# A round trip through DRAM in larger pieces, and a projection one step later, in a fused attention and gMLP kernel

## The chip, the cores and the metric

The kernel runs on one core of one Trainium2 chip. Its engines run side by side and are ordered by semaphores: TensorE (PE in the profile; PEld is its weight load), VectorE (DVE), ScalarE (ACT), GpSimd (POOL) and SyncE (SP), which here only issues DMAs. Every transfer between DRAM and the on-chip memory SBUF goes over the core's 16 DMA engines. TensorE writes to PSUM, which has eight banks. The metric is the device time in microseconds, as the median of several runs.

## The reference

Two branches work on the same layer-normalised input of 2048 rows and 512 columns, and the result is `x + s * silu(B)`. Everything is float32.

```
xn = layernorm(x)
q  = xn @ wq                       # 32 heads of 128; softmax over the last 512 cached keys
p  = softmax(q k^T / sqrt(128));   s = concat_h(p v) @ wo
z  = gelu(xn @ w_in);  z1, z2 = halves of 688;  z2 = layernorm(z2)
B  = (z1 * (w_sp @ z2 + b_sp)) @ w_out
out = x + s * silu(B)
```

## The kernel before, in words

*Precision.* Each float32 operand of a product is split into a high part and a rest. ACT casts the high part, and `rest` (L59) subtracts it on DVE or POOL. Each product is then three matmuls (`mm3`, L65 to L67): high by high, high by rest, rest by high.

*Blocks and steps.* The attention works on 128 blocks. A block is one head with 512 queries (function `where`). Each block has four steps of 128 queries, so the main loop over `t` runs through 512 steps, with some before and after. Each step carries work of several blocks at different stages. The offsets in L34 to L36 say how many steps apart the stages are. With `b` a block:

- `score(t)`, at step 4b+j: the three matmuls of q k^T, the row maximum on DVE (L475) and the exponential on ACT (L477), into `prob`.
- `turn(t)`, one step later: DVE transposes `prob` in blocks of 32 by 32 (L486).
- After the transposes the order within the 32-by-32 blocks is right, but the blocks of 32 partitions have to change places. This is done by a round trip through DRAM: a store into `p_dram` (L491) and, in `turned(b)`, loads into a tile `pL` (L499), four of them, each for 32 partitions.
- `shares(b, c)`, at step 4b+11+c: ACT and POOL split a quarter of `pL` into high part and rest.
- `pv(b, c)`, at step 4b+13+c: three matmuls of p v for that quarter, into one PSUM bank for the whole block. `pv_out` then copies and splits it (`oT`).
- `outp(b, j)`, at step 4b+18+j: the product with `wo`, added by DVE to `sacc` (L536).

*The q projection.* After the first four blocks, q is computed for groups of four blocks (two heads and two halves of 1024 rows) by a scheme with seven products in place of eight. A group has 42 matmuls (L448) spread over 16 steps. Group g begins at step 16g - `LEAD`. It needs three PSUM accumulators, a, b and c (`BANK`), and temporary tiles `qs` in SBUF; `q_evict` and `q_done` move the results to `qT` on ACT, DVE and, for one of the four, POOL. The rest of the fourth, read straight from bank a, is the DVE instruction of L728 (it is called from the list `late` at the end of a step).

*What sets the order.* The order of instructions on each engine is that of the program; each engine works strictly in that order. Within a step PE does `score`, `q_products`, `pv`, `outp`. In a step ACT does `shares` first, then the exponential. Buffers come from pools of a fixed number, and an instruction that opens a new tile waits until the last reader of the old one is done. The pool `ps_acc` has four PSUM banks, shared by the p v accumulators and by a, b, c of q.

*SP's queue.* All stores and loads of p, the heads' weights (`raw`, `wq`) and the pieces of x go through SP, in program order, and a DMA that waits holds all behind it. The heads' weights are issued six steps ahead.

*Other tiles.* `rawx` (pool `xq`) holds rows of the second half of x while they are normalised, transposed and stored to DRAM as operands for later groups (`later_x`, L309 for one of its casts), and later some columns of `w_in`. `pL` also holds the first columns of `w_in` at the start.

After the attention, the kernel computes z2 and the gMLP branch. The change doesn't touch that stage.

Of the kernel before, what the change touches and what calls it, by code (L numbers as in the profile page):

```python
# [8 lines left out]
F32 = mybir.dt.float32  # L9
# [8 lines left out]
P = 128  # L18
# [10 lines left out]
NBLK = H * NQ  # L29
# [3 lines left out]

XL, QL, ML, PL, OL = 11, 7, 11, 13, 18  # L34
T8 = NT // 2
LEAD = 13  # L36
Q = 32


# [1 line left out]
def mixer_kernel(ctx: ExitStack, tc: tile.TileContext, x, wh, w_in, w_sp, b_sp, w_out, out):  # L41
# [8 lines left out]
    nc = tc.nc  # L50
# [3 lines left out]
    dram = ctx.enter_context(tc.tile_pool(name="dram", bufs=1, space=DRAM))  # L54
# [3 lines left out]
    def rest(engine, lo, whole, hi):  # L58
        engine.tensor_tensor(lo, whole, hi.bitcast(F32), op=OP.subtract)  # L59

    late = []
# [23 lines left out]
    att = ExitStack()  # L85
    sp = att.enter_context(tc.tile_pool(name="sp", bufs=1))
    ap = att.enter_context(tc.tile_pool(name="ap", bufs=2))
    wq = att.enter_context(tc.tile_pool(name="wq", bufs=2))
    zs = att.enter_context(tc.tile_pool(name="zs", bufs=2))
    xq = att.enter_context(tc.tile_pool(name="xq", bufs=4))  # L90
    sacc = sp.tile([P, T8, D], F32, name="sacc")


# [3 lines left out]
    raw, wt = {}, {}  # L97

    def load_piece(key, k):
        n = NB if key[0] == "w" else 512  # L100
        r = raw[key, k] = (xq.tile([P, 512], F32, name="rawx") if key[0] == "w" else rawp.tile([P, 512], F32, name="raw"))
        nc.sync.dma_start(r[:, :n], (w_in if key[0] == "w" else wh)[key[1] % H, :, k])

    def load_early(n, cs):
        if (n, "raw") not in raw:
            raw[n, "raw"] = ap.tile([P, 16, P], F32, name="pL").rearrange("p k q -> p (k q)")
        for lo, hi in cs:
            nc.sync.dma_start(raw[n, "raw"][:, lo * NB:hi * NB].rearrange("p (c f) -> p c f", f=NB), w_in[n, :, lo:hi])
            for k in range(lo, hi):
                raw[("w", n), k] = raw[n, "raw"][:, k * NB:k * NB + NB]  # L110
# [91 lines left out]
    def ln_flip(i, parts=1):  # L202
        n, j = divmod(i, 4)
        if j == 0:
            for h in range(2):
                X[0][h, n] = block()
        if parts == 1:
            ps = flip(sacc[:, i, :])
        else:
            ps = ps_step.tile([P, NC, P], F32, name="ps_3")  # L210
        rests, rest_of = [], []
        for h in range(2):
            if parts > 1:
                for c in (2 * h, 2 * h + 1):
                    nc.tensor.transpose(ps[:, c, :], sacc[:, i, c * P:(c + 1) * P], ident)
            hi, lo = (quarter(X[0][h, n][:, a], j) for a in range(2))
            nc.scalar.copy(hi, ps[:, 2 * h:2 * h + 2])
            rests.append((lo, ps[:, 2 * h:2 * h + 2], hi))
        if n == 1:
            p2, y = ps.rearrange("p c q -> p (c q)"), sacc[:, i, :]  # L220
            nc.scalar.copy(y[:, :256], p2[:, :256])
            rest_of.append((y[:, 256:], p2[:, 256:], y[:, :256]))
        if parts > 1:
            return rests
        for r in rests:
            rest(nc.vector, *r)
        for r in rest_of:
            nc.vector.tensor_tensor(*r, op=OP.subtract)
# [131 lines left out]
    def z1_piece(i, n, between=lambda: None):  # L360
        z1_out(i, n, z1_product(i, n, between))


    pB = [None]
    qps, qT, pps, pD, pL, pT, oT, prob, sums = {}, {}, {}, {}, {}, {}, {}, {}, {}

    def where(b):
# [37 lines left out]
    def load_q(g):  # L405
        r = wraw[g] = wq.tile([P, 2, 512], F32, name="wq", bufs=2)
        h = 2 * g % H
        for k in range(2):
            nc.sync.dma_start(r[:, k], wh[h + k, :, 0])
# [41 lines left out]
    def q_evict(g, k):  # L451
        ps = qps[g, BANK[k]]
        if k in (0, 2, 3):
            t = qps[g, "t", k] = ap.tile([P, 512], F32, name="qs", bufs=2)
            nc.scalar.activation(t, ps, AF.Copy, scale=SCALE)  # L455
        elif k in (1, 5):
            nc.vector.scalar_tensor_tensor(ps, ps, SCALE, qps[g, "t", {1: 0, 5: 2}[k]], op0=OP.mult, op1=OP.add)
        elif k == 4:
            t = qps[g, "t", 3]
            nc.vector.scalar_tensor_tensor(t, ps, SCALE, t, op0=OP.mult, op1=OP.add)  # L460
# [18 lines left out]
    def turn(t):  # L479

        b, j = divmod(t, 4)
        if j % 2 == 0:
            pB[0] = ap.tile([P, 4, 2, P], F32, name="pB", bufs=3)
        nc.vector.transpose(pB[0][:, :, j % 2, :].rearrange("p a (c q) -> p a c q", q=Q),  # L486
                            prob.pop(t).rearrange("p (a c q) -> p a c q", a=4, q=Q))
        if j == 0:
            pD[b] = dram.tile([2, P, 1024], F32, name="p_dram", bufs=3)
        if j % 2:  # L490
            nc.sync.dma_start(pD[b][j // 2], pB[0].rearrange("p a j f -> p (a j f)"))  # L491
        if j == 3:
            nc.vector.reciprocal(sums[b], sums[b])

    def turned(b):
        pL[b] = ap.tile([P, 8, 256], F32, name="pL")
        of = pD.pop(b).rearrange("s (i r) (a f) -> a r (s i) f", i=4, a=4)
        for a in range(4):
            nc.sync.dma_start(pL[b][Q * a:Q * a + Q], of[a])  # L499

    def shares(b, c):
        hi = ap.tile([P, 512], F32R, name="pT_h", bufs=4)
        lo = ap.tile([P, 512], F32R, name="pT_l", bufs=4)
        p = pL[b].rearrange("p i (j f) -> p (i j) f", j=2)[:, :, Q * c:Q * c + Q]
        h, l = (t.rearrange("p (i q) -> p i q", q=Q) for t in (hi, lo))
        nc.scalar.copy(h, p)  # L506
        rest(nc.vector if 4 * b + c >= NSTEP - 10 and c % 2 else nc.gpsimd, l, p, h)
        pT[b, c] = (hi, lo)
# [6 lines left out]
    def pv_out(b, c):  # L515
        if c == 3:
            hi = ap.tile([P, 512], F32R, name="oT_h")
            lo = ap.tile([P, 512], F32R, name="oT_l")
            ps = pps.pop(b).rearrange("p (s i j q) -> p s i j q", s=2, i=4, j=2)
            h, l = (t.rearrange("p (s j i q) -> p s i j q", s=2, i=4, j=2) for t in (hi, lo))  # L520
            nc.scalar.copy(h, ps)
            for k in range(2):
                late.append((rest, nc.vector, l[:, k], ps[:, k], h[:, k]))
            oT[b] = (hi, lo)

    def outp(b, j):
# [44 lines left out]
    for g in range(1, NG):  # L571
        t0 = 16 * g - LEAD
        loads.setdefault(max(T0, t0 - 12), []).append(g)
# [20 lines left out]
    for k, d in enumerate((4, 6, 8, 11, 13, 15, 17)):  # L594
        for n in range(4):
            ends.setdefault(16 * (NG // 2 - 1) - LEAD + d + (0, 0, 1, 1)[n], []).append((fetch_part, 1, ORDER[k], n))
    ends.setdefault(16 * (NG - 1) - LEAD + 9, []).append((fetch_x, 1, (0, 1)))
    for k in ((0, 0), (1, 0)):
        ends.setdefault(NSTEP + 6, []).append((fetch_x, 0, k))
    n = 0  # L600
    for p in range(4):
        seq, store = later_x(p)
        for f, ks in seq:
            t = 30 + 13 * n // 5
# [41 lines left out]
    ps = ps_step.tile([P, 512], F32, name="ps_3")  # L646
# [9 lines left out]
    ps = ps_step.tile([P, 512], F32, name="ps_3")  # L656
# [4 lines left out]
    ps = ps_acc.tile([P, 512], F32, name="ps_a")  # L661
# [18 lines left out]
    for t in range(T0, T1):  # L680
        for key in loads.get(t, ()):
            if isinstance(key, int):
                load_q(key)
            else:
                load_piece(*key)
        bq, cq = divmod(t + QL, 4)
        bm, cm = divmod(t - ML, 4)
        bp, cp = divmod(t - PL, 4)
        bo, jo = divmod(t - OL, 4)
        i = t + XL  # L690
        if i < T8:
            ln_flip(i)
        if 0 <= bm < NBLK:
            shares(bm, cm)
        for f, args in todo.get(t, ()):
            f(*args)
        if 0 <= t < NSTEP:
            score(t)
        if i + 2 < T8:
            ln_apply(rows[i + 2], i + 2)  # L700
        if t in FILL:
            z1_piece(*FILL[t])
        if 0 <= bq < 4:
            qproj(bq, cq)
        g, s = divmod(t + LEAD, 16)
        if 0 < g < NG:
            q_products(g, s)
        if 0 <= bp < NBLK:
            pv(bp, cp)
        if 0 <= bo < NBLK:  # L710
            outp(bo, jo)
        if t in DRAIN:
            ps = z1_product(*DRAIN[t])
        if 0 <= bq < 4:
            qproj_out(bq, cq)
        for f, *args in q_events.get(t, ()):
            f(*args)
        if 0 <= bp < NBLK:
            pv_out(bp, cp)
        if t in DRAIN:  # L720
            z1_out(*DRAIN[t], ps)
        if 0 <= t - 1 < NSTEP:
            turn(t - 1)
        if t % 4 == 3 and 0 <= t // 4 - 1 < NBLK:
            turned(t // 4 - 1)
        while late:
            f, *args = late.pop(0)
            f(*args)  # L728
        for f, *args in ends.get(t, ()):
            f(*args)  # L730

    split_piece(("w", 2), 3, nc.vector)
    ps = z1_product(*LAST[-1])
# [276 lines left out]
```

## Time and profile before

| quantity | value |
|---|---|
| median of 3 runs | 1907.47 us (1906.44 to 1908.14) |
| profiled execution | 1907.01 us, its span 1905.1 us |
| mean granted clock of TensorE | 0.991 |
| DMA packets, data | 277624, 429.16 MB |

The span is the time from the first to the last instruction of the profiled execution. Busy times are of that execution. A row of waits gives the engine and line that waited, what it waited for, the total, how often, and the longest. A wait for several semaphores is put down to the one that came last. Lines (L486) are those of the kernel before.

### The profile page before, as it was taken

Reading aid. Unit: us, or ns where it says so; the run is one execution under the profiler, and the core shown is the slowest. Engines: PE = TensorE matmul, PEld = TensorE weight load, DVE = VectorE, ACT = ScalarE, POOL = GpSimd, SP = SyncE. Lnnn points to the kernel's source line nnn. Section 1 sums busy time; section 2 is a strip of 40 time slices with the busy share of each in tenths; the row PEclk is TensorE's granted clock in tenths of the full one; section 3 lists DMA queues with packets and bytes.
Section 4 is the critical chain, followed back from the end, with each engine's and each line's share of the span. In section 5 each row is a group of like instructions: output and inputs, shape, how many; then the busy total and the mean of one; then the engine's idle time right before and its main releaser. Section 6 shows DMA issues by size and latency. Waiting matters only on the chain.

```text
span 1905.1 us, 28198 instructions
## 1 busy us (share of the span) xinstructions
PE 1820.5 (96%) x8658; PEld 1540.4 (81%) x8658; DVE 1403.3 (74%) x2497; ACT 1179.1 (62%) x2631; POOL 1244.3 (65%) x1185
## 2 busy tenths in 40 slices
PE   8898999999999898999999999999999999999999
PEld 7776777777787686778887877878777899999998
DVE  5687888888888787788888888888888556333433
ACT  4666677777677575667677777777677545333422
POOL 3686798798798786788878888888888435000000
PEclk9998999999999999999999999999999999999999
DMA  5798999999999889999889899988999833545543
GB/s 180 198 282 228 237 264 242 251 265 239 252 264 244 216 248 296 267 270 247 236 239 241 241 241 245 245 237 245 236 246 260 257 134 119 194 146 168 158 134 96
DMA packets 277624, 429.16 MB, mean 225 GB/s; under 512 B 22272, under 2 KB 183808, under 8 KB 276320
## 3 DMA queue, kind: packets, MB, share of 16 engines
q1 hardware_dynamic: 272864, 421.72, 79.4%
q10 hardware_dynamic: 4608, 5.64, 0.8%
q8 instruction: 68, 1.11, 0.3%
q14 instruction: 84, 0.69, 0.1%
HBM read 260.55 MB, written 166.72 MB: 224 GB/s over the span
## 4 chain that ended last, share of the span: by engine, by line
PE 73%; DMA 11%; DVE 7%; ACT 3%; POOL 3%; issue 2%; SPq 1%; ACTq 0%; POOLq 0%; DVEq 0%
PE ps_a L448 11%; PE ps L65 9%; PE ps L67 9%; PE ps L66 9%; PE ps_a L65 7%; PE ps_a L66 6%; PE ps_a L67 6%; DMA pL<-p_dram 4%; PE ps_g L66 4%; PE ps_g L67 4%; PE ps_g L65 4%; DMA p_dram<-pB 2%; DVE sacc L536 2%; DVE pB L486 1%; ACT prob L477 1%
## 5 line engine op out<-in xcount | busy, mean ns | idle before, releaser
L59 POOL TENSOR_TENSOR pT_l<-pL,pT_h 128x512 fp32r<-128x512 f32 x507 | 657.9, 1298 | 265.5 <-ACT pT_h L506 250.7
L477 ACT ACTIVATE prob<-ps,nm 128x512 f32<-128x512 f32 x512 | 352.8, 689 | 290.9 <-DVE nm L475 285.1
L536 DVE SCALAR_TENSOR_TENSOR sacc<-ps,sums,sacc 128x512 f32<-128x512 f32 x496 | 369.6, 746 | 149.2 <-PE ps L67 144.2
L506 ACT CAST pT_h<-pL 128x512 fp32r<-128x512 f32 x512 | 318.1, 621 | 130.8 <-DMA pL<-p_dram 68.3
L448 PE MATMUL ps_a<-x,x 128*128 128x512 f32 x1302 | 378.6, 391 | 7.9 <-ACT qs L455 6.9
L486 DVE STREAM_TRANSPOSE pB<-prob 128x512 f32<-128x512 f32 x512 | 359.0, 701 | 23.2 <-ACT prob L477 22.4
L475 DVE TENSOR_REDUCE nm<-ps 128x1 f32<-128x512 f32 x512 | 338.8, 662 | 8.6 <-PE ps L67 8.5
L448 PEld LDWEIGHTS ps_a<-x,x 128*128 128x128 f32 x1302 | 245.9, 189 | 61.9 <-ACT qs L455 8.3
L59 POOL TENSOR_TENSOR wl<-raw,wh 128x512 fp32r<-128x512 f32 x192 | 249.2, 1298 | 9.0 <-ACT wh L141 9.0
L65 PE MATMUL ps_a<-pT_h,wh 128*128 128x512 f32 x512 | 204.2, 399 | 46.7 <-DVE qT_l L728 42.3
L65 PE MATMUL ps<-wh,qT_h 128*128 128x512 f32 x512 | 204.0, 399 | 8.6 <-DVE sacc L536 5.1
L66 PE MATMUL ps_a<-pT_l,wh 128*128 128x512 f32 x512 | 203.0, 396 | 7.3 <-POOL pT_l L59 7.1
L67 PE MATMUL ps_a<-pT_h,wl 128*128 128x512 f32 x512 | 200.9, 392 | 0.0
L66 PE MATMUL ps<-wl,qT_h 128*128 128x512 f32 x512 | 200.9, 392 | 0.0
L65 PE MATMUL ps<-wh,oT_h 128*128 128x512 f32 x512 | 200.7, 392 | 0.0
L66 PE MATMUL ps<-wl,oT_h 128*128 128x512 f32 x512 | 200.6, 392 | 0.0
L67 PE MATMUL ps<-wh,oT_l 128*128 128x512 f32 x512 | 200.6, 392 | 0.0
L67 PE MATMUL ps<-wh,qT_l 128*128 128x512 f32 x512 | 200.6, 392 | 0.0
L66 PE MATMUL ps_g<-z_l,x 128*128 128x344 f32 x512 | 162.1, 317 | 1.3 <-POOL z_l L59 1.3
L65 PE MATMUL ps_g<-z_h,x 128*128 128x344 f32 x512 | 162.1, 317 | 0.0
L67 PE MATMUL ps_g<-z_h,x 128*128 128x344 f32 x512 | 161.9, 316 | 0.0
L65 PEld LDWEIGHTS ps_a<-pT_h,wh 128*128 128x128 f32 x512 | 96.7, 189 | 79.2 <-DVE qT_l L728 55.0
(203 smaller groups left out, 3235.3 us busy)
## 6 DMA issues: line engine op xcount, KB each, us to landing
p_dram<-pB SPq DMA_DIRECT2D x256, 512.0 KB, 5.2
pL<-p_dram SPq DMA_DIRECT2D x512, 256.0 KB, 5.8
raw<-wh SPq DMA_DIRECT2D x194, 256.0 KB, 6.7
wq<-wh SPq DMA_DIRECT2D x62, 256.0 KB, 6.1
x<-w_sp SPq DMA_DIRECT2D x60, 256.0 KB, 6.0
x_dram<-rawx SPq DMA_DIRECT2D x32, 256.0 KB, 5.6
x<-x_dram SPq DMA_DIRECT2D x28, 256.0 KB, 7.6
u_dram<-uB SPq DMA_DIRECT2D x15, 384.0 KB, 2.3
```

What stands on the lines that cost most here:

```text
L59: engine.tensor_tensor(lo, whole, hi.bitcast(F32), op=OP.subtract)
L65: nc.tensor.matmul(ps, lh, rh, start=first, stop=False)
L66: nc.tensor.matmul(ps, lh, rl, start=False, stop=False)
L67: nc.tensor.matmul(ps, ll, rh, start=False, stop=last)
L448: nc.tensor.matmul(qps[g, bank], wt["q", g, k][a][:, c * P:(c + 1) * P], X[g * 2 // H][ORDER[k]][:, b, c], start=first, stop=r == 5, skip_ ...
L475: nc.vector.tensor_reduce(nm, ps, axis=AX.X, op=OP.max, negate=True)
L477: nc.scalar.activation(prob[t], ps, AF.Exp, bias=nm, accum_out=sums[b][:, j:j + 1])
L486: nc.vector.transpose(pB[0][:, :, j % 2, :].rearrange("p a (c q) -> p a c q", q=Q), prob.pop(t).rearrange("p (a c q) -> p a c q", a=4, q=Q))
L506: nc.scalar.copy(h, p)
L536: nc.vector.scalar_tensor_tensor(at, ps, rs, at, op0=OP.mult, op1=OP.add)
```

## The change

- p is transposed into one tile `pL` per block (four buffers of it; the tile `pB` goes). The store is one DMA per block, after the fourth transpose, of 128 rows of 8 KB; it used to be two, of rows of 4 KB.
- The loads go back into the same tile. The segment that already stands in its place isn't loaded. So there are six DMAs per block in place of four, in pieces of 2 KB in place of 1 KB, and a quarter less data.
- The loads are issued at step 4b+6; they used to be issued at step 4b+7.
- The columns of p now come in the order of queries, so that `pv_out` has one subtraction of 512 columns in place of two of 256.
- `LEAD` goes from 13 to 12: each q group, with its weights, sums and splits, begins one step later.
- `qs` has three buffers in place of two, `xq` five in place of four.
- The scratch reserved for descriptors of software DMAs is 4 KB in place of its default.

```diff
-LEAD = 13
+LEAD = 12
...
-    xq = att.enter_context(tc.tile_pool(name="xq", bufs=4))
+    xq = att.enter_context(tc.tile_pool(name="xq", bufs=5))
...
-            raw[n, "raw"] = ap.tile([P, 16, P], F32, name="pL").rearrange("p k q -> p (k q)")
+            raw[n, "raw"] = ap.tile([P, 16, P], F32, name="pL", bufs=4).rearrange("p k q -> p (k q)")
...
-            t = qps[g, "t", k] = ap.tile([P, 512], F32, name="qs", bufs=2)
+            t = qps[g, "t", k] = ap.tile([P, 512], F32, name="qs", bufs=3)
...
         b, j = divmod(t, 4)
-        if j % 2 == 0:
-            pB[0] = ap.tile([P, 4, 2, P], F32, name="pB", bufs=3)
-        nc.vector.transpose(pB[0][:, :, j % 2, :].rearrange("p a (c q) -> p a c q", q=Q),
+        if j == 0:
+            pL[b] = ap.tile([P, 4, 512], F32, name="pL", bufs=4)
+        nc.vector.transpose(pL[b][:, :, j * P:j * P + P].rearrange("p a (c q) -> p a c q", q=Q),
                             prob.pop(t).rearrange("p (a c q) -> p a c q", a=4, q=Q))
-        if j == 0:
-            pD[b] = dram.tile([2, P, 1024], F32, name="p_dram", bufs=3)
-        if j % 2:
-            nc.sync.dma_start(pD[b][j // 2], pB[0].rearrange("p a j f -> p (a j f)"))
         if j == 3:
+            pD[b] = dram.tile([4, Q, 4, 512], F32, name="p_dram", bufs=3)
+            nc.sync.dma_start(pD[b].rearrange("i r a f -> (i r) (a f)"), pL[b].rearrange("p a f -> p (a f)"))
             nc.vector.reciprocal(sums[b], sums[b])
 
     def turned(b):
-        pL[b] = ap.tile([P, 8, 256], F32, name="pL")
-        of = pD.pop(b).rearrange("s (i r) (a f) -> a r (s i) f", i=4, a=4)
+        of = pD.pop(b).rearrange("i r a f -> a r i f")
         for a in range(4):
-            nc.sync.dma_start(pL[b][Q * a:Q * a + Q], of[a])
+            for lo, hi in ((0, a), (a + 1, 4)):
+                if lo < hi:
+                    nc.sync.dma_start(pL[b][Q * a:Q * a + Q, lo:hi], of[a, :, lo:hi])
...
-        p = pL[b].rearrange("p i (j f) -> p (i j) f", j=2)[:, :, Q * c:Q * c + Q]
+        p = pL[b].rearrange("p i (j f) -> p (i j) f", j=4)[:, :, Q * c:Q * c + Q]
...
-            ps = pps.pop(b).rearrange("p (s i j q) -> p s i j q", s=2, i=4, j=2)
-            h, l = (t.rearrange("p (s j i q) -> p s i j q", s=2, i=4, j=2) for t in (hi, lo))
+            ps = pps.pop(b).rearrange("p (i j q) -> p i j q", i=4, j=4)
+            h, l = (t.rearrange("p (j i q) -> p i j q", i=4, j=4) for t in (hi, lo))
             nc.scalar.copy(h, ps)
-            for k in range(2):
-                late.append((rest, nc.vector, l[:, k], ps[:, k], h[:, k]))
+            late.append((rest, nc.vector, l, ps, h))
...
-        if t % 4 == 3 and 0 <= t // 4 - 1 < NBLK:
+        if t % 4 == 2 and 0 <= t // 4 - 1 < NBLK:
             turned(t // 4 - 1)
...
-    nc = bacc.Bacc("TRN2", target_bir_lowering=False, num_devices=1)
+    nc = bacc.Bacc("TRN2", target_bir_lowering=False, num_devices=1, dynamic_dma_scratch_size=4096)
```

More of the change, by code (lines that the diff above doesn't have):

```diff
@@ L361, in z1_piece @@
         z1_out(i, n, z1_product(i, n, between))
-    pB = [None]
     qps, qT, pps, pD, pL, pT, oT, prob, sums = {}, {}, {}, {}, {}, {}, {}, {}, {}
```

## The prediction

> **What bounds the kernel now.** First the busy shares on the page, then the same by stretches of the span: launch and first projections, the attention steps, the closing gMLP stage.
>
> ```profile
> span 1905.1 us, 28198 instructions
> 0.00:60.00 60.00, 52.92 (x304) 47.72 (x305) 34.88 (x77) 29.69 (x77) 25.71 (x42) 1.00 0.46 160
> 60.00:1480.00 1420.00, 1348.89 (x5820) 1090.90 (x5819) 1177.96 (x2100) 984.44 (x2294) 1157.27 (x1088) 0.99 0.92 249
> 1480.00:1905.00 425.00, 418.67 (x2538) 401.75 (x2536) 190.41 (x323) 165.00 (x262) 61.31 (x56) 1.00 0.48 156
> 700.00:800.00 100.00, 88.37 (x362) 70.38 (x362) 72.82 (x129) 60.38 (x141) 70.77 (x67) 0.95 1.00 279
> 900.00:1000.00 100.00, 98.07 (x430) 80.39 (x431) 85.65 (x153) 69.81 (x163) 82.96 (x78) 1.00 0.89 241
> 1700.00:1800.00 100.00, 100.00 (x612) 96.65 (x612) 36.26 (x62) 33.69 (x45) 0.00 (x0) 1.00 0.49 160
> ```
>
> The columns are the stretch, busy time and count of PE, PEld, DVE, ACT and POOL, then the granted clock, DMA share and GB/s. The change touches the attention steps, 60 to 1480 us. PE sets the pace there and idles 1420 - 1348.9 = 71.1 us; that, and what the clock loses after stalls, is all there is to win. The DMA engines are the second bound: 92% over the stage, 100% in 700:800, where PE issues 362 matmuls and not 430. DVE, POOL and ACT are busy 83%, 81% and 69%.
>
> Next, whom PE waits for (us in total, times, longest), and two rows of ACT's and one of SP's waits:
>
> ```profile
> PE ps_a L65 <- DVE qT_l L728: 42.3, 30, 7.8
> PE ps_a L66 <- POOL pT_l L59: 7.1, 13, 1.1
> PE ps_a L448 <- ACT qs L455: 6.9, 2, 6.3
> PE ps L65 <- DVE sacc L536: 6.4, 10, 1.3
> PE ps_a L65 <- ACT pT_h L506: 4.4, 3, 1.8
> PE ps L65 <- ACT prob L477: 3.1, 2, 2.5
> ACT pT_h L506 <- DMA pL<-p_dram: 68.3, 26, 8.0
> ACT rawx L309 <- DMA x_dram<-rawx: 22.5, 4, 8.1
> SPq L499 <- DMA p_dram<-pB: 145.0, 64, 8.1
> ```
>
> The first row is three fifths of PE's idle time, 30 waits for 31 groups of q. But the matmul at L65 (first p v product of a block) does not read qT_l. It opens a new accumulator, so it waits for a bank of ps_acc. The timeline of PE and DVE at one such wait:
>
> ```profile
> 1029.13 0.61 PE L448 MATMUL ps_a<-x,x 128*128 128x512 f32 x2
> 1030.71 0.50 PE L65 MATMUL ps_a<-pT_h,wh 128*128 128x512 f32 x1 [0.97 <-DVE qT_l L728]
> 1028.65 0.75 DVE L536 SCALAR_TENSOR_TENSOR sacc<-ps,sums,sacc 128x512 f32<-128x512 f32 x1 [0.78 <-PE ps L67]
> 1029.32 0.70 DVE L486 STREAM_TRANSPOSE pB<-prob 128x512 f32<-128x512 f32 x1
> 1030.00 0.66 DVE L728 SCALAR_TENSOR_TENSOR qT_l<-ps_a,qT_h 128x512 fp32r<-128x512 f32 x1
> ```
>
> PE is done at 1029.74 and DVE frees the bank at 1030.66, since that last read of bank a stands behind the previous step's sacc and transpose. In the calm part nearly every such wait is this 0.97.
>
> **The change, part by part.**
>
> *q a step later.* I followed the four banks by hand, oldest freed bank first. With a lead of 13, at step 5 of each 16 the q product b and the p v accumulator both open; one bank was freed four steps earlier, the other two (bank a of the old group, the previous block's accumulator) only in step 4. The p v product gets bank a, as the trace shows. With 12, b opens at step 6 and the p v product at step 5 takes a bank freed three steps ago; the youngest bank taken anywhere was freed two steps ago. So 30 x 0.97 = 29.1 us goes. The rest of that row, 42.3 - 29.1 = 13.2, is a few waits in which DVE and ACT were themselves late behind DMA.
>
> Moved with it by one step: each group's sums and splits (POOL, ACT), 42 products (PE), evictions (ACT, DVE), its two q loads, and in one group the 28 x loads. Relative to one another they stay. The shortest deadline is that of the qT of each group's second block, written by DVE and used by a score:
>
> ```profile
> 1022.64 0.69 DVE L59 TENSOR_TENSOR qT_l<-ps_a,qT_h 128x512 fp32r<-128x512 f32 x1
> 1028.45 0.39 PE L65 MATMUL ps<-wh,qT_h 128*128 128x512 f32 x1
> ```
>
> Ready at 1023.33, used at 1028.45: 5.1 us, and 2.5 after a step of 2.65 is taken away. POOL: by counting the rests per step, its worst backlog falls rather than rises (q sums no longer meet in two steps running). I book between 0 and 31 x 0.97 = 30 us for a new wait per group and take 5, because all margins I find exceed two microseconds.
>
> *Third qs buffer, fifth xq buffer.* The four ACT waits on L309 are the T2 piece asking for a buffer whose store was issued in the same step. With five there is one whose store is over. The 6.3-us PE wait on qs follows the longest of them (8.1). Gain 0 to 6.9; I take 6.3.
>
> *p's round trip.* The rows:
>
> ```profile
> p_dram<-pB SPq DMA_DIRECT2D x256, 512.0 KB, 5.2
> pL<-p_dram SPq DMA_DIRECT2D x512, 256.0 KB, 5.8
> raw<-wh SPq DMA_DIRECT2D x194, 256.0 KB, 6.7
> x_dram<-x SPq DMA_DIRECT2D x4, 1024.0 KB, 8.0
> sacc<-x SPq DMA_DIRECT2D x1, 1024.0 KB, 9.8
> out<-s_t SPq DMA_DIRECT2D x15, 256.0 KB, 2.3
> out<-s_t SPq DMA_DIRECT2D x2, 128.0 KB, 1.7
> 1009.39 0.40 SPq L491 DMA_DIRECT2D p_dram<-pB  x1
> 1015.90 2.26 SPq L499 DMA_DIRECT2D pL<-p_dram  x4
> 1025.30 0.62 ACT L506 CAST pT_h<-pL 128x512 fp32r<-128x512 f32 x1 [0.49 <-POOL pT_l L59]
> ```
>
> Bytes: 2.10 MB per block becomes 1.05 stored + 0.79 loaded = 1.84. Pieces: 1024 loads of 1 KB become 384 of 2 KB. DMA load: the quiet stretch 1700:1800, mostly 2-KB rows, moves 160 GB/s at a share of 0.49, 327 at full; 900:1000 moves 241 at 0.89, 271 at full. At 9.5 blocks per 100 us the stage then needs 22.4 MB per 100 us (17.4 of p, 5.0 of the rest), a share between 0.68 (at 327) and 0.83 (at 271). In 700:800, 362 matmuls at 46.5 a block are 7.8 blocks, 16.4 of the 27.9 MB; the other 11.5 and p for 9.2 blocks (16.9) need 87 to 105 us. I lean to the pieces mattering and take 0.72 in calm windows.
>
> The Trainium skill ("DMA: Bandwidth & Descriptors", section "Why small descriptors are slow (HBM only)") gives about 3 extra cycles per packet of 32-byte beats; as an estimate 35 cycles for 1 KB and 67 for 2 KB, so that larger pieces save only 4%. By it the share would be about 0.80, 700:800 would stay full, and the time that of the second rival below, 1875. No run here yet shows which holds.
>
> Latency: store issued at 1009.39, last load issued at 1018.16, ACT reads at 1025.30: 15.9 us are to be had, of which today 6.5 + 2.3 + a median 5.8 = 14.6 are used. The loads now follow the store's landing alone, in step 4b+6 and not 4b+7, past the raw loads that step 4b+7 issues. The store of twice the size lands between 5.2 and 8.0; 5.2 plus half a megabyte at 271 GB/s (1.9) is 7.1 under today's traffic and I take 6. Six issues at 0.45 are 2.7. The last piece lands between 1.7 and 5.8 later; I take 4.5. Sum 13.2, ends 9.6 and 16.5. SP gains 256 load issues (+115 us) and loses 128 stores (-42 at 0.33), hidden in its 145 us of waits on p's store and its longer ones on DVE. Behind the blocked load in SP's queue stand the next steps' raw loads: issued six steps (16 us) ahead, landing in 6.7, they can bear the some 6 us. The old loads also needed a pL buffer of two; with four they no longer wait for POOL. A transpose at step 4b+1 writes a buffer last read at 4b-2, so DVE does not wait.
>
> What this is worth to PE: of the 13.2 us above two thirds, 8.8; of POOL pT_l, sacc, pT_h and prob together (7.1 + 6.4 + 4.4 + 3.1 = 21.0) a third, 7.0, ends 0 and 21. After long stalls the clock is down:
>
> ```profile
> 154.00:158.00 4.00, 3.60 (x9) 2.84 (x10) 2.24 (x5) 3.21 (x8) 4.00 (x6) 0.50 1.06 238
> 158.00:162.00 4.00, 4.00 (x17) 3.27 (x16) 2.44 (x5) 1.59 (x4) 3.57 (x3) 0.89 0.48 189
> ```
>
> 26 matmuls in 8 us where 35 fit at 0.227: 2.0 us. Three stalls are that long, 6 us; I take 5.
>
> *The rest costs nothing.* One rest of 128x512 for two of 128x256:
>
> ```profile
> L59 DVE TENSOR_TENSOR oT_l<-ps_a,oT_h 128x256 fp32r<-128x256 f32 x256 | 95.0, 412 | 50.3 <-ACT oT_h L521 50.2
> L59 DVE TENSOR_TENSOR qT_l<-ps_a,qT_h 128x512 fp32r<-128x512 f32 x62 | 42.9, 691 | 5.0 <-ACT qT_h L381 1.5
> ```
>
> saves 128 x (824 - 691) ns = 17 us of DVE, off the path (DVE idles 242 us of the stage). Transposes and copies keep their shapes. The smaller DMA scratch changes addresses only; all data queues on the page are hardware ones.
>
> **Sum** against the profiled execution (1907.0 us; the median of the runs, 1907.5, is 0.5 above): 29.1 + 8.8 + 6.3 + 7.0 + 5.0 - 5.0 = 51.2. 1907.5 - 51 = 1856.
>
> **The rivals.** *The banks only change places:* the p v product, or a score waiting for its later qT, pays 0.97 per group elsewhere. Against it: the margins above. Time 1856 + 29 - 5 for the allowance = 1880. *DMA is not relieved:* bytes count, not pieces. Then 8.8, 7.0 and most of the 5.0 fall away, 1875; for it, 700:800 is full at 279 GB/s, above the 271 I started from. *All idle goes:* 71 + 6 less 2, 1832. *Slower, p comes late:* the whole megabyte starts only after the fourth transpose, while half of it used to be on its way two steps before. ACT is in order: a late pL holds the exp behind it, hence the transposes, hence the store of the block after next. That loop has 8 steps, 21.1 us, less 1.8 for cast, exp and transpose: 19.3 for the round trip. Beyond it each microsecond costs half of one per block, 64 on the run; from 20.1 it eats the gain. With 8.0 + 2.7 + 9.8 = 20.5 (the landings of the two one-megabyte rows) it gives 1856 + 77 = 1933. Against it: both rows stem from crowded stretches, and traffic falls.
>
> **How the numbers follow.** Forecast 54%, all idle gone 8, DMA not relieved 14, banks only moved 11, nothing moves 3, p late 10. Faster is 54 + 8 + 14 + 11 = 87; 0.2% is 3.8 us, about what a measurement can tell from no change. The range 1836 to 1884 leaves out p late, no change and half of "all idle gone", 17 to 20%.
>
> **What would show it.** The wait of L65 on L728 gone or under 5 us, no other PE row above 10; PE idle in 60:1480 near 25; ACT's wait on pL under 25 and on x_dram under 5; 128 stores of p at about 6 us, 768 loads near 4.5; DMA share near 0.72 in calm windows and under 1.00 in 700:800. It is wrong if ACT waits for pL in every block, or if a bank wait of about 1 us per group stands on another row.

## The result, and the profile after

The changed kernel takes 1829.1 us (median of four runs, 1825.1 to 1829.4). The kernel before takes 1907.0 us beside it. The ratio is 0.959, with a 95% interval of 0.957 to 0.961. The gain is 78 us, where 51 was forecast, and the time lies just below the range given.

First the page of the changed kernel, then PE's longest waits, one row of ACT's and two of SP's. Its lines differ from those of before: L447 was L448, L485 was L486, L497 was L499, L504 was L506, L533 was L536.

```profile
span 1827.1 us, 28750 instructions
PE 1799.5 (98%) x8658; PEld 1540.9 (84%) x8658; DVE 1395.8 (76%) x2369; ACT 1175.7 (64%) x2631; POOL 1244.6 (68%) x1185
DMA packets 181372, 395.65 MB, mean 217 GB/s; under 512 B 24320, under 2 KB 54784, under 8 KB 163680
```

```profile
PE ps_a L65 <- ACT pT_h L504: 8.1, 2, 4.3
PE ps L65 <- DVE sacc L533: 4.3, 7, 1.1
PE ps_a L66 <- POOL pT_l L59: 4.1, 8, 0.8
ACT pT_h L504 <- DMA pL<-p_dram: 13.0, 6, 7.6
```

```profile
SPq L497 <- DMA p_dram<-pL: 477.2, 126, 7.7
SPq L489 <- DVE sums L490: 187.3, 87, 17.9
```

The 42.3-us row of L65 on the q rest is gone. So are the row on qs and ACT's 22.5 us on x_dram; ACT's wait on p's loads fell from 68.3 to 13.0 us. The span fell by 78.0 us. PE's idle time fell by 57.0 of them (1905.1 - 1820.5 = 84.6 to 1827.1 - 1799.5 = 27.6). The other 21.0 came from PE's *busy* time (1820.5 to 1799.5), with the same 8658 matmuls. That part I had booked at five.

The same stretch of the calm second half, in both kernels (columns as before: stretch, busy time and count of PE, PEld, DVE, ACT, POOL, clock, DMA share, GB/s). Before:

```profile
900.00:1400.00 500.00, 488.75 (x2134) 399.11 (x2135) 427.68 (x755) 353.67 (x820) 416.93 (x388) 1.00 0.90 241
```

After:

```profile
900.00:1400.00 500.00, 499.14 (x2201) 412.30 (x2200) 441.18 (x737) 367.97 (x855) 436.44 (x402) 1.00 0.76 226
```

In 500 us PE issues 67 matmuls more, which is 15.2 us at their 0.227 us. Its idle time fell by 10.4 us only.

p's transfers after the change (KB each, median us from issue to landing):

```profile
p_dram<-pL SPq DMA_DIRECT2D x128, 1024.0 KB, 5.1
pL<-p_dram SPq DMA_DIRECT2D x256, 192.0 KB, 3.9
pL<-p_dram SPq DMA_DIRECT2D x256, 128.0 KB, 3.8
pL<-p_dram SPq DMA_DIRECT2D x256, 64.0 KB, 3.8
```

The store of double size lands as fast as the half one did (5.2), and the loads land in 3.9 us where they took 5.8.

What is left is two stalls in crowded stretches. One is of 3.8 us, ending at 144 us; the row of windows right behind it:

```profile
145.00:149.00 4.00, 3.44 (x9) 2.62 (x9) 1.75 (x4) 3.51 (x9) 4.00 (x5) 0.50 0.32 104
```

The granted clock is 0.50 throughout these four microseconds. The Trainium skill ("TensorE: Matmul & The Clock Gate", "Part 1: The HAM clock gate (the "warmup" mystery)") says that the clock falls to half after an idle window of about 3.4 us. The 3.8-us stall fits that, and the clock is 1.00 in a stretch with stalls of 0.97 us only, the row of before above. But the length of one stall does not decide it here, and the measurement goes before the rule: the clock was also 0.50 behind stalls of 2.9 and 2.7 us in the run of the round trip alone (below) and behind stalls of 1.8 and 0.8 us in a row in the first thinned-out run, and it stayed at 1.00 behind one of 2.5 us in the kernel before.

### The profile page after: what moved, and what is told of

It is laid out like the page before. It is cut to its first block, busy times and chain, and to the rows that moved or that the text cites. A ratio compares the mean times of both kernels' runs of the same rounds, so it can differ in the third digit from the quotient of the medians.

```text
span 1827.1 us, 28750 instructions
## 1 busy us (share of the span) xinstructions
PE 1799.5 (98%) x8658; PEld 1540.9 (84%) x8658; DVE 1395.8 (76%) x2369; ACT 1175.7 (64%) x2631; POOL 1244.6 (68%) x1185
## 4 chain that ended last, share of the span: by engine, by line
PE 91%; DMA 5%; DVE 1%; POOL 1%; ACT 1%; issue 1%; SPq 0%; ACTq 0%; POOLq 0%; DVEq 0%
PE ps_a L447 15%; PE ps L65 12%; PE ps L67 12%; PE ps L66 12%; PE ps_a L66 8%; PE ps_a L67 8%; PE ps_a L65 8%; PE ps_g L66 4%; PE ps_g L65 4%; PE ps_g L67 4%; DMA p_dram<-pL 2%; DMA pL<-p_dram 1%; PE ps_f L65 1%; PE ps_f L66 1%; PE ps_f L67 1%; DMA raw<-wh 1%
## 5 line engine op out<-in xcount | busy, mean ns | idle before, releaser
L533 DVE SCALAR_TENSOR_TENSOR sacc<-ps,sums,sacc 128x512 f32<-128x512 f32 x496 | 369.8, 746 | 126.2 <-PE ps L67 120.5
L447 PE MATMUL ps_a<-x,x 128*128 128x512 f32 x1302 | 376.6, 390 | 0.0
L485 DVE STREAM_TRANSPOSE pL<-prob 128x512 f32<-128x512 f32 x512 | 358.9, 701 | 16.2 <-ACT prob L476 16.2
L504 ACT CAST pT_h<-pL 128x512 fp32r<-128x512 f32 x512 | 318.3, 622 | 46.0 <-DMA pL<-p_dram 13.0
L447 PEld LDWEIGHTS ps_a<-x,x 128*128 128x128 f32 x1302 | 244.9, 188 | 51.4 <-PE ps L67 0.3
L65 PE MATMUL ps_a<-pT_h,wh 128*128 128x512 f32 x512 | 200.5, 392 | 8.1 <-ACT pT_h L504 8.1
L65 PE MATMUL ps<-wh,qT_h 128*128 128x512 f32 x512 | 201.2, 393 | 3.2 <-DVE sacc L533 3.2
L65 PE MATMUL ps<-wh,oT_h 128*128 128x512 f32 x512 | 199.8, 390 | 0.0
L65 PE MATMUL ps_g<-z_h,x 128*128 128x344 f32 x512 | 162.1, 317 | 0.0
L59 POOL TENSOR_TENSOR x<-wq,x 128x256 fp32r<-128x256 f32 x186 | 138.7, 746 | 1.5 <-ACT x L429 1.5
```

The costliest lines, as they stand in the source:

```text
L65: nc.tensor.matmul(ps, lh, rh, start=first, stop=False)
L447: nc.tensor.matmul(qps[g, bank], wt["q", g, k][a][:, c * P:(c + 1) * P], X[g * 2 // H][ORDER[k]][:, b, c], start=first, stop=r == 5, skip_ ...
L485: nc.vector.transpose(pL[b][:, :, j * P:j * P + P].rearrange("p a (c q) -> p a c q", q=Q), prob.pop(t).rearrange("p (a c q) -> p a c q", a ...
L533: nc.vector.scalar_tensor_tensor(at, ps, rs, at, op0=OP.mult, op1=OP.add)
```

## The experiments

The questions were which of the three parts (the q step, the buffers, the round trip of p) had brought the time, and why it was more than the sum of their rows. After the result the leading theory was that a wait of PE costs more than its idle row.

### Each part by itself

*The q step alone*, on the kernel before:

```diff
-LEAD = 13
+LEAD = 12
```

> The kernel before with LEAD 12 and nothing else. Theory A (a wait of PE costs its idle row and about 0.25 us more, because the matmuls around a gap start 0.26 us further apart than their idle row says): the 30 waits of L65 on L728 at 0.97 us go, 30 x 1.22 = 37 us, so about 1870. Theory B (the idle row is all that a wait costs): 1907 - 29 = 1878. Theory C (the banks only change places): 1900 or more, with a row of about 1 us per group elsewhere. In all three the long stalls behind late p loads (7.8 and 5.9 us in the kernel before) remain, on another row.

Measured: 1853.5 us, ratio 0.972 (0.971 to 0.974). This is 54.6 us less, more than any of the theories had. The waits of L65 on L728 are gone, and no row of some thirty waits stands in their place. A few long waits do: L65 on ACT's pT_h has 8.7 us in place of 4.4, and one wait of 5.5 us on oT_h is new. In all PE idles 40.6 us less over the span, and is busy 13.1 us less. Its calm stretch:

```profile
900.00:1400.00 500.00, 500.00 (x2207) 414.18 (x2206) 444.20 (x783) 368.26 (x856) 436.03 (x403) 1.00 0.93 250
```

PE is busy without a gap, with 73 matmuls more than before. That is 16.5 us of work, where only 11.25 us had been idle. The DMA share is 0.93, *higher* than before, and PE does not notice. So in calm stretches the crowded DMA engines cost nothing, and the bank wait was nearly all of the loss.

*The q step undone*, on the changed kernel:

```diff
-LEAD = 12
+LEAD = 13
```

> The changed kernel with LEAD back at 13. Theory A: 30 bank waits of 0.97 us come back at 1.22 each, 1829 + 37 = 1866. Theory B: 1829 + 29 = 1858. Rival: with p in time DVE runs earlier and the bank is free by itself, at most 1835.

Measured: 1863.3 us, ratio 0.977 (0.975 to 0.978); 34 us of the gain are lost. The wait is back, thirty times, now with a total of 32.9 us and 4.6 at most (it had been 42.3 and 7.8):

```profile
PE ps_a L65 <- DVE qT_l L725: 32.9, 30, 4.6
```

The step is worth 54.6 us alone and 34.2 beside the other parts. My reading is that with p late the bank wait also passes on the lateness of ACT and DVE. The two rows show 9.4 us of that (42.3 less 32.9); what the other 11 are is not shown.

*The bank alone.* With LEAD 13, bank a of each group is read out a step earlier, so that it is free when the p v product opens:

```diff
             elif k == 6:
-                q_events.setdefault(t0 + done + 2, []).append((q_done, g, k))
+                q_events.setdefault(t0 + done + 1, []).append((q_done, g, k))
```

> The kernel before, LEAD 13, with bank a of each q group read out and freed one step earlier (step 3 of 16 in place of 4), so that the p v product of step 5 finds a bank freed two steps ago. LEAD 12 alone gave 1853, 54 us less, while the idle row of that wait was only 42, and 443 matmuls per 100 us in calm windows against 430. Theory A (the bank wait is the cause, and costs more than its row): most of the 54 us comes, 1853 to 1862, and calm windows hold 440 or more matmuls. Theory D (a good part of it was another meeting: the third eviction of a group and the copy of oT fell into one step of ACT with LEAD 13, and made a score wait): the bank part alone is 30 x 1.22 = 37 us, 1870, and calm windows stay at about 437.

Measured: 1869.2 us, ratio 0.980 (0.978 to 0.982), so 40 us of the 54.6. Neither theory holds alone. In the calm stretch PE has 2200 matmuls, nearly the 2207 of the q step:

```profile
900.00:1400.00 500.00, 499.62 (x2200) 412.20 (x2199) 442.78 (x784) 367.26 (x855) 435.16 (x405) 1.00 0.93 250
```

There the bank is nearly the whole cause, 66 of the 73 matmuls. The other 15 us lie mostly in the first 300 us (957 matmuls in 60 to 300, against 1002 with the q step). In the crowded stretches a bank freed two steps ago was still too late twice:

```profile
PE ps_a L65 <- DVE qT_l L728: 10.5, 2, 6.0
```

Which of the other things that the q step moves saves them was not tried.

*The round trip alone* (with the single subtraction and the small scratch): the changed kernel with three lines as before.

```diff
-LEAD = 12
+LEAD = 13
...
-    xq = att.enter_context(tc.tile_pool(name="xq", bufs=5))
+    xq = att.enter_context(tc.tile_pool(name="xq", bufs=4))
...
-            t = qps[g, "t", k] = ap.tile([P, 512], F32, name="qs", bufs=3)
+            t = qps[g, "t", k] = ap.tile([P, 512], F32, name="qs", bufs=2)
```

> Only the new round trip of p (one store, 2-KB loads, own segment not loaded, step 4b+6, four pL buffers); LEAD 13, four xq and two qs buffers as before. Theory A: the bank waits remain, and some 8 us of the buffer stalls: 1829 + 37 + 8 = 1874, so the trip by itself is worth about 33 us. Rival (the trip alone is worth little, because bank waits hide what it frees): 1890 or more.

Measured: 1873.5 us, ratio 0.982 (0.981 to 0.983): 34.5 us, as expected.

*The buffers alone* (with the small scratch that makes room), on the kernel before:

```diff
-    xq = att.enter_context(tc.tile_pool(name="xq", bufs=4))
+    xq = att.enter_context(tc.tile_pool(name="xq", bufs=5))
...
-            t = qps[g, "t", k] = ap.tile([P, 512], F32, name="qs", bufs=2)
+            t = qps[g, "t", k] = ap.tile([P, 512], F32, name="qs", bufs=3)
```

> The kernel before with five xq buffers, three qs buffers and the 4-KB scratch that makes room. Theory: ACT's four waits of L309 on x_dram go and with them the 6.3-us stall of PE and its slow clock, 1907 - 9 = 1898. Rival: the stall is only a late DMA and moves to another row, 1904 to 1907. If the scratch itself does anything, the time leaves both.

Measured: 1894.7 us, ratio 0.993 (0.991 to 0.995): 13 us, a little more than the theory's 9. The five runs lie further apart than those of other kernels here (1890.1 to 1901.5). ACT's row on x_dram and PE's 6.3-us wait on qs are gone.

*The q step and the buffers*, on the kernel before: the two diffs above together.

> The kernel before with LEAD 12, five xq and three qs buffers and the small scratch; p's round trip as before. What is left to the changed kernel is then the round trip's worth once the bank wait is gone. Theory (the trip's worth is in the crowded stretches only: first 300 us and the 28 loads of x): 1840 to 1846, so 11 to 17 us for the trip, half of the 34.5 it gave with the bank waits in place. Rival (the trip's worth is independent of the rest): 1829 + 34 = 1863, more than LEAD 12 alone, which can hardly be.

Measured: 1836.0 us, ratio 0.962 (0.960 to 0.964). The buffers bring 17.5 us on top of the q step. The whole round trip is left with 7 us, and its interval just overlaps that of the changed kernel (0.957 to 0.961). By the traces they lie in the crowded stretches: 17 matmuls more in 60 to 300 us and 14 in 700 to 800. This is the main finding: alone the three parts give 54.6, 34.5 and 13.3, together 102, and in company 78. The buffers lose nothing in company (13.3 alone, 17.5 on top of the q step, 10.2 on top of the trip), so it is the q step and the trip whose gains are in part the same. The bank by itself accounts for 40 of the q step's 54.6; whether the trip overlaps with these or with the other 15, no run tells.

*Which buffer:* the changed kernel with the old number of xq buffers.

```diff
-    xq = att.enter_context(tc.tile_pool(name="xq", bufs=5))
+    xq = att.enter_context(tc.tile_pool(name="xq", bufs=4))
```

> The changed kernel with four xq buffers. Both buffer changes together were worth 13 us with LEAD 13 and 17.5 us with LEAD 12. Theory: all of it is the fifth xq buffer, ACT's four waits of L309 on x_dram come back (20 us of ACT) with one or two stalls of PE of 4 to 6 us and slow clock behind them: 1829 + 15 = 1844. Rival: the third qs buffer carries half: 1837 or less.

Measured: 1845.1 us, ratio 0.967 (0.965 to 0.969), 16 us more than the changed kernel. ACT's four waits are back, and nearly the whole worth of the buffers is this one; the third qs buffer was not tried by itself. The row of ACT's waits, and the two longest of PE's new ones:

```profile
ACT rawx L309 <- DMA x_dram<-rawx: 20.3, 4, 7.4
PE ps_a L447 <- ACT qs L454: 3.1, 1, 3.1
PE ps L65 <- ACT prob L476: 2.4, 1, 2.4
```

PE's two hold 5.5 us of the 16. In all PE idles 8.1 us more than in the changed kernel (35.7 and 27.6) and is busy 7.0 us longer: here too the loss is larger than the idle time.

### What in the round trip matters

*The own segment loaded too,* on the changed kernel: four loads of 256 KB, the bytes of before.

```diff
         for a in range(4):
-            for lo, hi in ((0, a), (a + 1, 4)):
-                if lo < hi:
-                    nc.sync.dma_start(pL[b][Q * a:Q * a + Q, lo:hi], of[a, :, lo:hi])
+            nc.sync.dma_start(pL[b][Q * a:Q * a + Q], of[a])
```

> The changed kernel, but each group's own segment is loaded too: four loads of 256 KB in 2-KB pieces, 2.10 MB per block as before the change. If the spared bytes matter: DMA share in calm windows 0.82 and more, ACT waits longer for pL in the first 300 us and around 730 us, 1832 to 1838. If PE is covered anyway: 1829, within 3 us; two DMA issues fewer per block speak for a small gain.

Measured: 1902.5 us, ratio 0.997 (0.995 to 0.998). Neither expectation foresaw this: 73 us lost by a third more of load (1.05 MB per block, not 0.79), although the q step and the buffers with the old trip move the same bytes at 1836. The views that explain it are SP's waits, p's store and its queue in time:

```profile
SPq L495 <- DMA p_dram<-pL: 859.6, 127, 9.5
SPq L489 <- DVE sums L490: 23.5, 5, 18.1
```

```profile
p_dram<-pL SPq DMA_DIRECT2D x128, 1024.0 KB, 8.4
```

```profile
1002.35 0.38 SPq L489 DMA_DIRECT2D p_dram<-pL  x1
...
1010.89 1.75 SPq L495 DMA_DIRECT2D pL<-p_dram  x4
...
1013.16 0.43 SPq L489 DMA_DIRECT2D p_dram<-pL  x1
1021.72 1.75 SPq L495 DMA_DIRECT2D pL<-p_dram  x4
1023.57 0.38 SPq L489 DMA_DIRECT2D p_dram<-pL  x1
...
1034.96 0.48 SPq L489 DMA_DIRECT2D p_dram<-pL  x1
```

SP issues the next store almost as soon as the loads are issued. It hardly waits for DVE any more: the row shown has 5 waits, not 87, and by all its rows the store waits for DVE 9.6 us in 900 to 1400, not 97.6. So the transposes are there in time, and the store is not held by a loop through ACT. It goes out while the loads still move and lands in 8.4 us, not 5.1; only then do the next loads go. From store to store it is 10.8, 10.4 and 11.4 us here, and 10.9 on average in 900 to 1400. At full pace PE needs 10.55 us for a block (46.5 matmuls at 0.227). So the queue has no slack, and ACT waits for pL:

```profile
ACT pT_h L502 <- DMA pL<-p_dram: 158.7, 77, 10.0
```

The chain of work that ended last says the same: p's store and loads have 25% of the span in it, where they have 3% in the changed kernel. That this queue sets the pace is read from the trace; no run undid it with the bytes kept.

*The same bytes as the changed kernel in 1-KB pieces:* each load cut in two.

```diff
                 if lo < hi:
-                    nc.sync.dma_start(pL[b][Q * a:Q * a + Q, lo:hi], of[a, :, lo:hi])
+                    for h in (0, 256):
+                        nc.sync.dma_start(pL[b][Q * a:Q * a + Q, lo:hi, h:h + 256], of[a, :, lo:hi, h:h + 256])
```

> The changed kernel with the same bytes, but each of the six loads of a block cut in two of 1-KB pieces: twelve loads. With the own segment loaded the time was 1902 and the store of p landed in 8.4 us, not 5.1, although the same bytes in the old order (two half stores, loads one store later) ran at 1836 with fuller DMA engines. Theory L (a round trip per block on SP's queue: store lands, loads are issued and moved, and only then does the next store move; it must stay under PE's 10.55 us per block): twelve issues take 5.3 us in place of 2.7 and 1-KB pieces move slower, so the next store falls behind the loads, lands in 8 us or more, and the time is 1880 or more with no byte added. Theory M (it was the added bytes): 1829 to 1840.

Measured: 2065.5 us, ratio 1.083 (1.080 to 1.086). No byte was added, so here it isn't bytes. The theory of SP's round trip holds in its direction and was wrong about the store, which lands in 5.5 us and not in 8 or more. The time is lost in the issuing:

```profile
1001.21 0.33 SPq L489 DMA_DIRECT2D p_dram<-pL  x1
1008.28 6.26 SPq L498 DMA_DIRECT2D pL<-p_dram  x12
1014.64 0.37 SPq L489 DMA_DIRECT2D p_dram<-pL  x1
...
1019.49 5.83 SPq L498 DMA_DIRECT2D pL<-p_dram  x12
...
1025.89 0.38 SPq L489 DMA_DIRECT2D p_dram<-pL  x1
```

```profile
900.00:1400.00 500.00, 459.26 (x1900) 360.19 (x1899) 381.46 (x633) 316.32 (x739) 374.39 (x348) 0.97 0.64 198
```

Twelve issues take about 6 us. With the landing before them, SP comes round only every 12.3 us on average in 900 to 1400 (13.4 and 11.2 in these rows), and the issuing of the loads has 10% of the span in the chain that ended last. The DMA engines are at 0.64 meanwhile, their lowest share in this stretch of any kernel here. This run changes pieces and issues together; pieces alone were not tried.

*The loads a step later,* on the changed kernel:

```diff
-        if t % 4 == 2 and 0 <= t // 4 - 1 < NBLK:
+        if t % 4 == 3 and 0 <= t // 4 - 1 < NBLK:
```

> The changed kernel with the loads at step 4b+7 in place of 4b+6. SP waits for the store's landing anyway and runs ahead of the other engines, so that only the weight loads of one step change sides: 1829, within 5 us. Rival (the earlier step is part of the gain): 1840 or more. By theory L weights that go before the loads make the round trip longer: a few us slower, not faster.

Measured: 1827.2 us, ratio 0.957 (0.955 to 0.960): no difference. SP gets there early and waits either way.

### Thinning out what is left

*The crowded stretches.* The three stores of 1 MB become quarters, at steps 100 to 122; the 28 loads of x go evenly over 20 steps.

```diff
-    for t, k in ((-2, (0, 1)), (22, (0, 0)), (25, (1, 0)), (28, (1, 1))):
-        ends.setdefault(t, []).append((keep_x, k))
-    for k, d in enumerate((4, 6, 8, 11, 13, 15, 17)):
-        for n in range(4):
-            ends.setdefault(16 * (NG // 2 - 1) - LEAD + d + (0, 0, 1, 1)[n], []).append((fetch_part, 1, ORDER[k], n))
+    ends.setdefault(-2, []).append((keep_x, (0, 1)))
+    for i in range(12):
+        ends.setdefault(100 + 2 * i, []).append((keep_part, ((0, 0), (1, 0), (1, 1))[i // 4], i % 4))
+    for i in range(28):
+        ends.setdefault(16 * (NG // 2 - 1) - LEAD + 4 + 20 * i // 28, []).append((fetch_part, 1, ORDER[i // 4], i % 4))
```

> The changed kernel, with its two crowded stretches thinned out: the three one-megabyte stores of x blocks at steps 22 to 28 become twelve quarters at steps 100 to 122, and the 28 loads of x blocks are issued evenly over 20 steps in place of 14. The two remaining long stalls of PE (3.8 us at 144 us and 4.3 us at 731 us, each with slow clock behind it) stand in these stretches. Theory: both shrink below 1 us, 1829 - 12 = 1817. Rival: the stalls come from elsewhere (SP's queue order, the pieces of the second half of x), 1826 to 1829.

Measured: 1822.2 us, ratio 0.955 (0.953 to 0.957): 7 us of the 12 hoped for. The stall at 144 us is gone; one of 1.8 us, ending at 724 us, stays.

*The same, right behind p's store:* the quarters and the x loads only in the steps in which a store of p is issued (every fourth).

```diff
-        ends.setdefault(100 + 2 * i, []).append((keep_part, ((0, 0), (1, 0), (1, 1))[i // 4], i % 4))
+        ends.setdefault(100 + 4 * i, []).append((keep_part, ((0, 0), (1, 0), (1, 1))[i // 4], i % 4))
     for i in range(28):
-        ends.setdefault(16 * (NG // 2 - 1) - LEAD + 4 + 20 * i // 28, []).append((fetch_part, 1, ORDER[i // 4], i % 4))
+        ends.setdefault(16 * (NG // 2 - 1) - LEAD + 4 + 4 * min(5, (i + 1) // 5), []).append((fetch_part, 1, ORDER[i // 4], i % 4))
```

> The thinned-out kernel (1822), with the x loads and the quarters of the x stores issued only in the step of p's store, right behind it in SP's queue, so that they move while the store's landing is awaited and are through before the loads of p. Theory L: the last stalls (1.8, 0.8 and 0.8 us around 730 us) go, 1817 to 1820. Rival: five x loads in a row hold the loads of p back and the stall grows, 1824 or more.

Measured: 1816.0 us, ratio 0.952 (0.950 to 0.955). It is the fastest of all, 13 us under the changed kernel; its interval and that of the first thinned-out run just overlap. No wait of PE in the attention is longer than about 1 us (one of 0.8 us stays at 731 us), and the mean granted clock is 1.000:

```profile
core 0: 1812.7 us, clock 1.000
```

```profile
PE ps L65 <- DVE sacc L536: 4.1, 7, 1.0
PE ps_a L66 <- POOL pT_l L59: 2.4, 4, 0.8
```

Five x loads in a row did not hold p's loads back, since they are issued while SP waits for the store's landing: p's loads begin 6.5 and 6.4 us after their store in two rounds with x loads, and 6.6 and 5.6 us after it in the next two rounds without.

## Why the prediction missed its range

The signs that the prediction named came: the row of L65 on L728 is gone, no other row of PE is above 10 us (8.1), PE idles about 17 us in 60 to 1480 where 25 was expected, ACT waits 13.0 us for pL, the store lands in 5.1 us and the loads in 3.9. What failed is the price. Taken one on top of the other, the q step, the buffers and the trip brought 54.6, 17.5 and 7 us, where 24.1 (with the allowance), 6.3 and 20.8 were booked.

*The q step, 29.1 us.* This is the step of the prediction that failed. The mechanism was right: the bank, its place, and that a lead of 12 removes the wait without another wait of each group taking its place. The size was wrong. I priced each wait at its idle row, 0.97 us, 30 times. That left out the busy time around the waits, of which 13.1 us went with the q step alone, and the row's excess, which I gave to the trip. The bank alone brought 40 us, the q step 54.6; which of the things that move with it brings the other 15 stays open. By the calm stretch the loss was 16.5 us where 11.25 were idle, and with the bank alone 15.0 where 10.9 were idle, so 1.4 to 1.5 times the row. The timeline in the prediction shows part of it: the matmul before the gap is counted busy until its modelled end, and the one after it takes 0.50 us in place of 0.39. Beside the other parts the step is worth 34.2.

*The allowance of 5 us for a new wait.* Nothing came for it. The shortest deadline I named, the second block's qT, shows in no row of PE's waits.

*The xq and qs buffers, 6.3 us.* Right in mechanism, too small: 16 us for the fifth xq buffer. I counted the one long stall of PE behind an ACT wait. The others cost as well: with four buffers PE idles 8.1 us more and is busy 7.0 us longer.

*p's round trip, 8.8 + 7.0 + 5.0 us.* Too large: 7 us are left to it beside the other parts, though it brings 34.5 alone. I had split off the excess of the bank row (13.2 us) and given two thirds of it to the trip. The q step alone removes nearly the whole of that (PE idles 40.6 us less), and late p then costs far less. On top, the calm stretches have no use for free DMA engines: PE runs without a gap at a share of 0.93 in the q step alone, and idles 0.9 us in 500 at 0.76 after.

*The latency of the trip, 13.2 us.* 5.1 for the store, 2.67 for six issues and 3.9 for the last landing are 11.7, within the ends, and 1.5 below what I took.

*The DMA share, 0.72.* Measured 0.76 at 226 GB/s, 297 at full. The Trainium skill's rule on small descriptors ("DMA: Bandwidth & Descriptors", "Why small descriptors are slow (HBM only)") had given about 0.80 by my estimate. The truth lies between. At the same 241 GB/s the share is 0.90 in the kernel before and 0.83 with the own segment loaded (2-KB loads, 8-KB stores):

```profile
900.00:1400.00 500.00, 492.53 (x2134) 396.92 (x2133) 426.77 (x711) 352.09 (x825) 419.07 (x389) 1.00 0.83 241
```

That is 8% less for larger pieces at the same rate, more than the rule's 4% and less than I took. It did not matter for the time.

*The rivals.* The time is near that of "All idle goes" (1832, a chance of 8%), but that is luck: in 60 to 1480 us PE still idles about 17 us (71.1 before), and it priced what PE loses besides its idle time at 6 us, where 21.0 us of busy time went. "p late" I had sought in ACT's order, with 19.3 us for its loop. The narrow loop is SP's, store to store in a block's 10.55 us, and the changed kernel keeps clear of it by leaving out the own segment. I didn't see that loop; the two runs that lengthen it lost 73 and 236 us.

*The rest.* The sign was right. The step of the loads does not matter in the changed kernel, though I had described it as part of the gain. The single subtraction and the small scratch were booked at nothing; neither was tried by itself.

## What to carry to other kernels

A wait of the engine that sets the pace can cost more than its idle row, here 1.4 to 1.5 times in a calm stretch: compare how many instructions it issues in a calm stretch with and without the wait. Losses that several causes share must be priced by taking one part away at a time; here the parts' gains alone add up to 102 us for a change worth 78. Where a store and the loads that need it go through one queue each round, add up landing, issues and transfer on that queue and hold the sum against the round's time: here a third more load cost nearly everything gained and twice the issues more than that, with the DMA engines less busy than before.

## What the runs showed that I had not expected

By these traces a queue of DMAs set the pace while the DMA engines did not: shares of 0.83 and 0.64 went with 1902 and 2066 us, and a share of 0.93 with 1836. And four waits of ACT, which is busy 64% of the span, came back with a loss of 16 us, not much under their 20.
